# Two consecutive tokens per partition in a fused linear attention and soft mixture-of-experts kernel

## The chip, the cores and the metric

The kernel runs on one core of a Trainium2 chip. Time is device microseconds (us); a run counts as slow when it lies more than 1.5% above the fastest of the same kernel. Medians count all runs of a kernel, ratios its fast runs alone, so small differences are judged by the ratios. Profiles are one execution each; a span in a profile is some 1.8 us shorter than the timed value. In profiles PE is TensorE, PEld its weight loads, DVE VectorE, ACT ScalarE, POOL GpSimd, and SP the engine whose queue (SPq) issues the loads. Tiles lie in one of two on-chip memories, SBUF and PSUM; the kernel's matmuls write to PSUM. "Before" and "after" are the two versions of the kernel. A pair is the changed kernel's unit of 256 tokens, a chunk the earlier kernel's unit of 128.

## The reference

Shapes: r, k, v are 4 x 8 x 768 x 48 (batch, head, token, head dimension), f32; eight experts, four slots each, hidden width 1024. Cut to what matters:

```python
for t in range(S):                       # attention with a decaying state
    cur = einsum('bhd,bhe->bhde', u * k[t], v[t])
    y[t] = einsum('bhd,bhde->bhe', r[t], state + cur)
    state = w * state + einsum('bhd,bhe->bhde', k[t], v[t])
x = y as (3072 tokens) x (384)
logits = x @ phi                         # soft mixture of experts, 32 slots
d = softmax(logits, over tokens); slot_in = d.T @ x
slot_out[e] = relu(slot_in[e] @ w1[e]) @ w2[e]      # e = 0..7
return softmax(logits, over slots) @ slot_out
```

The softmax over tokens needs all tokens, so the experts can only start after the attention loop.

## The kernel before

The loop handles 24 chunks of 128 tokens, one token per partition. GpSimd multiplies r and k with powers of the decay and k with u; ScalarE copies v to bf16 and r into PSUM; TensorE transposes, computes 128x128 scores of each head, output and state; VectorE multiplies scores with the triangular mask, forms the diagonal term (ku, its sum, dv) and decays the state. All PSUM tiles are single, and in the timelines each engine ran its instructions in program order (VectorE from 60.51 us on: state multiply, ku, its sum, dv, mask multiplies). Weights of the experts come by sixteen transfers of 768 KB, issued from GpSimd in the iterations that W_AT names. Cuts are marked "# ...".

```python
def load_batch(b):                       # 192-byte rows: 48 f32 of one token and head
    # ...
    if b > 0:
        for t, (_, src) in zip(tiles, srcs):
            nc.sync.dma_start(out=t[:].rearrange("p h c d -> p (h c) d")[:, :, 0:D],
                              in_=src[b].rearrange("h (c p) d -> p (h c) d", p=C))
        return
    for c in range(nC):
        # one transfer of 128 tokens for each of r, k, v

def tables():
    for _ in range(C.bit_length() - 1):  # w to the power 128 by seven squarings
        nc.vector.tensor_mul(w_pd[:], w_pd[:], w_pd[:])
    for par in range(2):
        ps = slice(par * 64, par * 64 + 64)
        nc.vector.tensor_copy(wm[ps, :, par * D:(par + 1) * D],
                              w_pd[ps, :, None].to_broadcast([64, nP, D]))
    nc.vector.tensor_copy(phi_s[:], phi_f[:])

def mults(i):
    # ...
    nc.gpsimd.tensor_mul(rr[:, :, 0:D], r_b[:, :, c, 0:D], W_neg[:])
    nc.gpsimd.tensor_mul(kk[:, :, 0:D], k_b[:, :, c, 0:D], W_k3)
    nc.gpsimd.tensor_mul(ku[:], k_b[:, :, c, 0:D], u3)
    nc.scalar.copy(v_bf[:], v_b[:, :, c, 0:D])

def diag(i):
    nc.vector.tensor_mul(s["ku"][:], s["ku"][:], s["r_p"][:])
    # ... d: 8 sums per token, in PSUM
    nc.vector.tensor_reduce(d, s["ku"][:], axis=mybir.AxisListType.X, op=ALU.add)
    nc.vector.tensor_mul(dv[:], s["v"][:], d[:, :, None].to_broadcast([P, H, D]))

def att_a(i):
    for q in range(nP):
        for a in range(2):
            sl = slice(a * 64, a * 64 + 64)
            nc.tensor.matmul(at_p[a][:, q, :], t_s[sl, 1, q, :], t_s[sl, 0, q, :], # ...
    for a in range(2):
        nc.vector.tensor_mul(at_s[:, a, :, :], at_p[a][:], mask_ut[:, None, :].to_broadcast([P, nP, P]))
# att_b: dv and the state product into y_p, new state in sd_p; att_c: scores times v, x_t by ScalarE
# xt, lg: transposed x_t, logits, Exp; disp: dispatch sums into un_p; lexp_t: transposed logits

W_AT = [9, 10, 15, 15, 16, 16, 17, 18, 19, 20, 21, 22, 23, 24, 24, 24]
# ...
for i in range(nN + 3):                  # conditions on i left out
    att_a(i); mults(i + 2); trans(i + 1); att_b(i); r_copy(i + 1); xt(i - 1)
    disp(i - 2); att_c(i); diag(i + 1); lg(i - 1); lexp_t((i - 5) // G)
    # load_w for the entries of W_AT equal to i
# then the experts (up: h_p, down: so_p), the combination and twelve output transfers
```

The softmax here doesn't subtract the row's maximum and nothing guards it: scores larger than these inputs give would overflow.

Of the kernel before, what the change touches and what calls it, by code (L numbers as in the profile page):

```python
# [11 lines left out]
def kernel(  # L12
# [35 lines left out]
    nG = nN // G  # L48

# [3 lines left out]
    w2_all = wts.tile([P, E, nF, Dm], bf, name="w2_all")  # L53
    cst = ctx.enter_context(tc.tile_pool(name="cst", bufs=1))
    fill = cst.tile([P, 40], f32, name="fill")
    late = ExitStack()
    ld = late.enter_context(tc.tile_pool(name="ld", bufs=2))
# [3 lines left out]
    def load_batch(b):  # L61
        srcs = (("r_b", r), ("k_b", k), ("v_b", v))
        tiles = [ld.tile([P, H, nC, 64], f32, name=name, tag=name) for name, _ in srcs]
        loads[b] = tiles
        if b > 0:
            for t, (_, src) in zip(tiles, srcs):
                nc.sync.dma_start(out=t[:].rearrange("p h c d -> p (h c) d")[:, :, 0:D],  # L67
                                  in_=src[b].rearrange("h (c p) d -> p (h c) d", p=C))
            return
        for c in range(nC):  # L70
            for t, (_, src) in zip(tiles, srcs):
                nc.sync.dma_start(out=t[:, :, c, 0:D],  # L72
                                  in_=src[b, :, c * C:(c + 1) * C, :].rearrange("h p d -> p h d"))

    w_rep = cst.tile([P, H * D], f32, name="w_rep")
    nc.sync.dma_start(out=w_rep[:], in_=w.flatten().partition_broadcast(P))
    u_rep = cst.tile([P, H * D], f32, name="u_rep")
    nc.scalar.dma_start(out=u_rep[:], in_=u.flatten().partition_broadcast(P))
    load_batch(0)
# [6 lines left out]
    iotash = cst.tile([P, 1], mybir.dt.int32, name="iotash")  # L86
    nc.gpsimd.iota(iotash, pattern=[[0, 1]], base=-C, channel_multiplier=1)
    ishf = cst.tile([P, 1], f32, name="ishf")
    nc.vector.tensor_copy(ishf[:], iotash[:])
    ishf2 = cst.tile([P, 1], f32, name="ishf2")  # L90
    nc.vector.tensor_scalar(out=ishf2[:], in0=ishf[:], scalar1=-1.0, scalar2=-1.0,
                            op0=ALU.mult, op1=ALU.add)
    ident = cst.tile([P, P], bf, name="ident")
    make_identity(nc, ident)
    mask_ut = cst.tile([P, P], f32, name="mask_ut")
    make_upper_triangular(nc, mask_ut, val=1.0, diag=False)
# [6 lines left out]
    W_neg = cst.tile([P, H, D], f32, name="W_neg")  # L103
    nc.scalar.activation(out=warm[:], in_=warm[:], func=AF.Ln)
    nc.scalar.activation(out=w_rep[:], in_=w_rep[:], func=AF.Ln)
    nc.scalar.activation(out=W_neg[:].rearrange("p h d -> p (h d)"), in_=w_rep[:], func=AF.Exp, scale=ishf[:])  # L106
    nc.scalar.activation(out=w_rep[:], in_=w_rep[:], func=AF.Exp, scale=ishf2[:])

    wm = cst.tile([P, nP, D2], f32, name="wm")
    nc.vector.memset(wm[:], 0.0)  # L110
    ones = cst.tile([P, P], bf, name="ones")
    nc.vector.memset(ones[:], 1.0)
    phi_s = cst.tile([P, nM, ES], bf, name="phi_s")

    def tables():
        for _ in range(C.bit_length() - 1):
            nc.vector.tensor_mul(w_pd[:], w_pd[:], w_pd[:])
        for par in range(2):
            ps = slice(par * 64, par * 64 + 64)
            nc.vector.tensor_copy(wm[ps, :, par * D:(par + 1) * D],  # L120
                                  w_pd[ps, :, None].to_broadcast([64, nP, D]))
        nc.vector.tensor_copy(phi_s[:], phi_f[:])

    W_k3 = w_rep[:].rearrange("p (h d) -> p h d", h=H)
    u3 = u_rep[:].rearrange("p (h d) -> p h d", h=H)

    NB = 3
    rr_t, kk_t = [], []
    for i in range(NB):
        for lst, nm in ((rr_t, "rr"), (kk_t, "kk")):  # L130
            t = cst.tile([P, H, 64], bf, name=f"{nm}{i}")
            nc.vector.memset(t[:, :, D:64], 0.0)
            lst.append(t)
    st_t = [cst.tile([P, nP, D2], bf, name=f"st{i}") for i in range(2)]
# [3 lines left out]
    Lexp = cst.tile([P, nN, ES], bf, name="Lexp")  # L138
    LexpT = cst.tile([P, nG, P], bf, name="LexpT")
    rsum = cst.tile([P, nN], f32, name="rsum")  # L140
    rsum_r = cst.tile([P, nN], f32, name="rsum_r")

    def load_w(i):
        e = i // 2
        if i % 2 == 0:
            nc.gpsimd.dma_start(out=w1_all[:, e, :, :], in_=w1_ap[:, e, :, :])  # L146
        else:
            nc.gpsimd.dma_start(out=w2_all[:, e, :, :], in_=w2_ap[:, e, :, :])  # L148

    unsiT = cst.tile([P, nM, ES], bf, name="unsiT")  # L150
    csum_r = cst.tile([P, ES], f32, name="csum_r")

    with tc.tile_pool(name="wk", bufs=2) as wk, \
         tc.tile_pool(name="wk3", bufs=3) as wk3, \
         tc.tile_pool(name="wk4", bufs=4) as wk4, \
         tc.tile_pool(name="ps", bufs=1, space=bass.MemoryType.PSUM) as ps:
        un_p = ps.tile([P, nM + 1, ES], f32, name="un_p")
        st8 = {}

        def mults(i):  # L160
            b, c = divmod(i, nC)
            if b not in loads:
                load_batch(b)
            if c == 1 and 1 <= b < B - 1:
                load_batch(b + 1)
            r_b, k_b, v_b = loads[b]
            rr, kk = rr_t[i % NB], kk_t[i % NB]
            nc.gpsimd.tensor_mul(rr[:, :, 0:D], r_b[:, :, c, 0:D], W_neg[:])  # L168
            nc.gpsimd.tensor_mul(kk[:, :, 0:D], k_b[:, :, c, 0:D], W_k3)  # L169
            ku = wk.tile([P, H, D], f32, name="ku")  # L170
            nc.gpsimd.tensor_mul(ku[:], k_b[:, :, c, 0:D], u3)  # L171
            v_bf = wk3.tile([P, H, D], bf, name="v_bf")
            nc.scalar.copy(v_bf[:], v_b[:, :, c, 0:D])  # L173
            st8[i] = dict(rr=rr, kk=kk, ku=ku, v=v_bf)

        def r_copy(i):
            b, c = divmod(i, nC)
            r_p = ps.tile([P, H, D], f32, name="r_p")
            nc.scalar.copy(r_p[:], loads[b][0][:, :, c, 0:D])  # L179
            st8[i]["r_p"] = r_p  # L180

        def diag(i):
            b, c = divmod(i, nC)
            s = st8[i]
            nc.vector.tensor_mul(s["ku"][:], s["ku"][:], s["r_p"][:])  # L185
            sd_p = ps.tile([P, nP * D2 + H], f32, name="sd_p")
            s["sd"] = sd_p
            d = sd_p[:, nP * D2:nP * D2 + H]
            nc.vector.tensor_reduce(d, s["ku"][:], axis=mybir.AxisListType.X, op=ALU.add)  # L189
            dv = wk.tile([P, H, D], bf, name="dv")  # L190
            nc.vector.tensor_mul(dv[:], s["v"][:], d[:, :, None].to_broadcast([P, H, D]))  # L191
            s["dv"] = dv

        def trans(i):
            s = st8[i]
            t_p = ps.tile([P, 2, nP, P], bf, name="t_p")
            for a, nm in enumerate(("rr", "kk")):
                for q in range(nP):
                    nc.tensor.transpose(t_p[:, a, q, :],  # L199
                                        s[nm][:, 2 * q:2 * q + 2, :].rearrange("p h d -> p (h d)"), ident[:])  # L200
            t_s = wk.tile([P, 2, nP, P], bf, name="t_s")
            nc.scalar.copy(t_s[:], t_p[:])  # L202
            s["t"] = t_s

        def att_a(i):
            s = st8[i]
            t_s = s["t"]
            at_p = [ps.tile([P, nP, P], f32, name=f"at_p{a}") for a in range(2)]
            for q in range(nP):
                for a in range(2):  # L210
                    sl = slice(a * 64, a * 64 + 64)
                    nc.tensor.matmul(at_p[a][:, q, :], t_s[sl, 1, q, :], t_s[sl, 0, q, :],  # L212
                                     start=(q == 0), stop=(q == nP - 1), skip_group_check=True)
            at_s = wk.tile([P, 2, nP, P], bf, name="at_s")
            for a in range(2):
                nc.vector.tensor_mul(at_s[:, a, :, :], at_p[a][:],  # L216
                                     mask_ut[:, None, :].to_broadcast([P, nP, P]))
            s["at"] = at_s

        def att_b(i):  # L220
            b, c = divmod(i, nC)
            s = st8[i]
            y_p = ps.tile([P, H * D], f32, name="y_p")
            s["y"] = y_p
            nc.tensor.matmul(y_p[:], ident[:], s["dv"][:].rearrange("p h d -> p (h d)"),  # L225
                             start=True, stop=False, skip_group_check=True)
            if c > 0:
                for q in range(nP):
                    nc.tensor.matmul(y_p[:, q * D2:(q + 1) * D2], s["t"][:, 0, q, :], st_t[i % 2][:, q, :],
                                     start=False, stop=False, skip_group_check=True)  # L230
# [12 lines left out]

        x_of = {}

        def att_c(i):
            s = st8[i]
            y_p = s["y"]
            for a in range(2):
# [57 lines left out]
        for i in range(nN + 3):  # L307
            if i < nN:
                att_a(i)
# [116 lines left out]
```

## Time and profile before

| what | before |
|---|---|
| time, median of 3 runs | 154.82 us (153.78 to 155.56) |
| first mask multiply starts | 19.5 us |
| last mask multiply ends | 107.4 us |
| first expert matmul starts | 111.4 us |
| last expert matmul ends | 135.6 us |
| span ends | 153.2 us |

The first mask multiply marks the end of the preparation and the last one the end of the loop. From the page of the kernel before: busy us (share of the span) and count of each engine; TensorE's granted clock in tenths over 40 equal slices; the shares of the chain that ended last, by engine.

```profile
PE 86.6 (57%) x1433; PEld 65.3 (43%) x1433; DVE 98.2 (64%) x206; ACT 77.7 (51%) x162; POOL 86.2 (56%) x100
...
PEclk9999999998555899999999655999755555555555
...
DMA 38%; SPq 21%; POOL 12%; PE 10%; ACT 6%; DVE 4%; issue 4%; ACTq 0%; DVEq 0%; POOLq 0%
```

VectorE's 64% is an average over a loop in which it is full (busy 20.35 of the 21 us from 60 to 81 us) and a weight wait in which it has little to do (6.44 of the 29.8 us from 105 us on). DMA and the queue that issues it (SPq) are 59% of the chain. These two readings lead to different hopes for a change: cheaper transfers, or fewer VectorE microseconds.

### The profile page before, as it was taken

What the parts mean: (1) busy time and instruction counts of PE and PEld (TensorE: products, weight loads), DVE (VectorE), ACT (ScalarE), POOL (GpSimd) and SP (SyncE); (2) the same over time, 40 slices, a digit from 0 to 9 for tenths busy, and PEclk for the clock granted to TensorE, in tenths of its full rate; (3) what the DMA queues carried; (4) which work ended last, traced back from release to release, by engine and by line L of the source; (5) the groups of instructions that cost most, each with busy time, mean ns of one, the idle gap of its engine ahead of it and who ended that gap; (6) DMA issues with size and microseconds to landing.
All of it is one profiled execution on the core that took longest, in us unless ns stands there. A gap on an engine that the chain in (4) does not pass through costs nothing.

```text
span 153.2 us, 3605 instructions
## 1 busy us (share of the span) xinstructions
PE 86.6 (57%) x1433; PEld 65.3 (43%) x1433; DVE 98.2 (64%) x206; ACT 77.7 (51%) x162; POOL 86.2 (56%) x100
## 2 busy tenths in 40 slices
PE   0035059782778878768783789785396522259100
PEld 0014047561656755546562577563296411132000
DVE  3009998992788899999994988999232100028610
ACT  3446126853767887897928777864300000018510
POOL 7089917784577789998899999995000000000000
PEclk9999999998555899999999655999755555555555
DMA  3999998964389929996899999999999999907994
GB/s 65 196 216 202 220 223 254 278 198 117 98 231 285 267 58 155 205 284 186 250 297 209 207 206 208 209 209 207 209 207 208 207 210 202 171 1 278 400 399 157
DMA packets 47873, 32.13 MB, mean 210 GB/s; under 512 B 19424, under 2 KB 44768, under 8 KB 47856
## 3 DMA queue, kind: packets, MB, share of 16 engines
q0 software_dynamic: 11616, 12.63, 49.0%
q1 hardware_dynamic: 36096, 19.07, 44.8%
q10 hardware_dynamic: 144, 0.20, 0.7%
q8 instruction: 11, 0.18, 0.5%
q14 instruction: 6, 0.05, 0.1%
HBM read 39.77 MB, written 4.72 MB: 290 GB/s over the span
## 4 chain that ended last, share of the span: by engine, by line
DMA 38%; SPq 21%; POOL 12%; PE 10%; ACT 6%; DVE 4%; issue 4%; ACTq 0%; DVEq 0%; POOLq 0%
DMA w_all<-in_moe_w_dram 20%; DMA v_b<-in_v_dram 14%; SPq L72 12%; SPq L67 10%; DMA out_dram<-o_s 4%; POOL rr L168 3%; PE t_p L199 3%; POOL kk L169 2%; POOL ku L171 2%; POOL w_all L148 2%; ACT t_s L202 2%; PE at_p L212 2%; ACT xt_s L267 1%; POOL w_all L146 1%; ACT r_p L179 1%
## 5 line engine op out<-in xcount | busy, mean ns | idle before, releaser
L202 ACT COPY t_s<-t_p 128x1024 bf16<-128x1024 bf16 x24 | 24.3, 1011 | 13.7 <-PE t_p L199 13.7
L171 POOL TENSOR_TENSOR ku<-k_b,u_rep 128x384 f32<-128x384 f32 x24 | 24.0, 1001 | 12.8 <-DVE sd_p L189 12.0
L216 DVE TENSOR_TENSOR at_s<-at_p,mask_ut 128x512 bf16<-128x512 f32 x48 | 30.7, 681 | 0.0
L168 POOL TENSOR_TENSOR rr<-r_b,W_neg 128x384 bf16<-128x384 f32 x24 | 24.1, 1004 | 4.4 <-ACT W_neg L106 4.2
L169 POOL TENSOR_TENSOR kk<-k_b,w_rep 128x384 bf16<-128x384 f32 x24 | 24.0, 1001 | 1.3 <-PE sd_p L238 0.7
L185 DVE TENSOR_TENSOR ku<-ku,r_p 128x384 f32<-128x384 f32 x24 | 13.1, 547 | 16.3 <-POOL ku L171 8.9
L393 ACT ACTIVATE o_s<-o_p,rsum_r 128x384 f32<-128x384 f32 x12 | 6.4, 584 | 29.9 <-PE o_p L387 27.9
L173 ACT CAST v_bf<-v_b 128x384 bf16<-128x384 f32 x24 | 12.2, 507 | 10.5 <-DMA v_b<-in_v_dram 10.5
L252 PE MATMUL y_p<-v_bf,at_s 128*128 128x48 bf16 x192 | 12.5, 194 | 7.5 <-DVE at_s L216 7.5
L199 PE MATMUL t_p<-ident,rr 128*128 128x128 bf16 x96 | 11.4, 254 | 9.3 <-POOL rr L168 9.3
L256 ACT CAST x_t<-y_p 128x384 bf16<-128x384 f32 x24 | 11.6, 484 | 5.7 <-PE y_p L252 5.7
L189 DVE TENSOR_REDUCE sd_p<-ku 128x8 f32<-128x384 f32 x24 | 13.5, 561 | 0.8
L191 DVE TENSOR_TENSOR dv<-v_bf,sd_p 128x384 bf16<-128x384 bf16 x24 | 13.3, 554 | 0.8
L267 ACT COPY xt_s<-xl_p 128x384 bf16<-128x384 bf16 x24 | 11.5, 481 | 4.0 <-PE xl_p L265 3.9
L225 PE MATMUL y_p<-dv,ident 128*128 128x384 bf16 x24 | 9.4, 394 | 6.5 <-DVE dv L191 6.3
L274 PE MATMUL xl_p<-phi_s,xt_s 128*128 128x32 bf16 x72 | 5.9, 185 | 12.2 <-ACT xt_s L267 11.7
L212 PE MATMUL at_p<-t_s 64*128 64x128 bf16 x192 | 11.4, 251 | 2.1 <-ACT t_s L202 2.1
L252 PEld LDWEIGHTS <-at_s 128*128 128x128 bf16 x192 | 8.5, 103 | 9.5 <-DVE at_s L216 8.6
L242 DVE TENSOR_TENSOR st<-sd_p,wm 128x384 bf16<-128x384 f32 x20 | 11.0, 550 | 1.6 <-PE sd_p L238 1.4
L199 PEld LDWEIGHTS <-rr 128*128 128x128 bf16 x96 | 6.5, 110 | 12.5 <-POOL rr L168 9.7
L179 ACT COPY r_p<-r_b 128x384 f32<-128x384 f32 x24 | 11.7, 489 | 0.0
L199 PE MATMUL t_p<-ident,kk 128*128 128x128 bf16 x96 | 11.5, 254 | 0.3 <-POOL kk L169 0.3
(66 smaller groups left out, 171.0 us busy)
## 6 DMA issues: line engine op xcount, KB each, us to landing
w_all<-in_moe_w_dram POOLq DMA_DIRECT2D x16, 768.0 KB, 15.0
out_dram<-o_s SPq DMA_DIRECT2D x12, 384.0 KB, 4.1
r_b<-in_r_dram SPq DMA_DIRECT2D x6, 192.0 KB, 3.6
k_b<-in_k_dram SPq DMA_DIRECT2D x6, 192.0 KB, 3.7
v_b<-in_v_dram SPq DMA_DIRECT2D x6, 192.0 KB, 3.7
u_rep<-in_u_dram ACTq DMA_DIRECT2D x1, 192.0 KB, 5.3
w_rep<-in_w_dram SPq DMA_DIRECT2D x1, 192.0 KB, 5.0
phi_f<-in_moe_phi_dram POOLq DMA_DIRECT2D x1, 48.0 KB, 4.6
```

The costliest lines, as they stand in the source:

```text
L67: nc.sync.dma_start(out=t[:].rearrange("p h c d -> p (h c) d")[:, :, 0:D], in_=src[b].rearrange("h (c p) d -> p (h c) d", p=C))
L72: nc.sync.dma_start(out=t[:, :, c, 0:D], in_=src[b, :, c * C:(c + 1) * C, :].rearrange("h p d -> p h d"))
L168: nc.gpsimd.tensor_mul(rr[:, :, 0:D], r_b[:, :, c, 0:D], W_neg[:])
L169: nc.gpsimd.tensor_mul(kk[:, :, 0:D], k_b[:, :, c, 0:D], W_k3)
L171: nc.gpsimd.tensor_mul(ku[:], k_b[:, :, c, 0:D], u3)
L189: nc.vector.tensor_reduce(d, s["ku"][:], axis=mybir.AxisListType.X, op=ALU.add)
L191: nc.vector.tensor_mul(dv[:], s["v"][:], d[:, :, None].to_broadcast([P, H, D]))
L199: nc.tensor.transpose(t_p[:, a, q, :], s[nm][:, 2 * q:2 * q + 2, :].rearrange("p h d -> p (h d)"), ident[:])
L202: nc.scalar.copy(t_s[:], t_p[:])
L212: nc.tensor.matmul(at_p[a][:, q, :], t_s[sl, 1, q, :], t_s[sl, 0, q, :], start=(q == 0), stop=(q == nP - 1), skip_group_check=True)
L216: nc.vector.tensor_mul(at_s[:, a, :, :], at_p[a][:], mask_ut[:, None, :].to_broadcast([P, nP, P]))
L252: nc.tensor.matmul(y_p[:, h * D:(h + 1) * D], s["at"][:, a, q, :], s["v"][:, h, :], start=False, stop=(a == 1 and q == nP - 1), skip_group ...
```

## The change

The intent: put two consecutive tokens of a head on one partition, so that a row of a load is 384 bytes instead of 192 and one load covers 256 tokens; keep chunks of 128 tokens, now on 64 partitions with two tokens each, so that scores are computed by 64x64 tiles of the array; hold logits per pair only, which frees memory for four sets of loads and for weights that come early. GpSimd's and ScalarE's instructions become twice as wide and half as many. Core of the diff, cuts marked "# ...":

```diff
+        t = ld.tile([P, H, J, D], f32, name=name)              # J = 2, four buffers
+        nc.sync.dma_start(out=t[:].rearrange("p h j d -> p h (j d)"),
+                          in_=src[b, :, i * TS:(i + 1) * TS, :].rearrange("h (p j) d -> p h (j d)", j=J))
 # ... decay tables and masks for both tokens of a partition
-            nc.gpsimd.tensor_mul(rr[:, :, 0:D], r_b[:, :, c, 0:D], W_neg[:])
+            nc.gpsimd.tensor_mul(rr[:, :, :, 0:D], jh(r_l), W_n[:])
 # ... kk, ku and v_bf likewise: 768 instead of 384 wide
+        def kur(n, j):
+            nc.vector.tensor_mul(s["ku"][:, j, :, :], s["ku"][:, j, :, :], s["rp"][:])
 # ... diag: one sum and one dv for 768 columns
-                    nc.tensor.matmul(at_p[a][:, q, :], t_s[sl, 1, q, :], t_s[sl, 0, q, :],
+                for g in range(2):
+                    for a in range(2):
+                        sl = slice(a * 64, a * 64 + 64)
+                        nc.tensor.matmul(at_p[a][g * HF:(g + 1) * HF, q, :], kT[sl, q, g, j, :],
+                                         rT[sl, q, g, :, :].rearrange("p j c -> p (j c)"),
+                                         start=True, stop=True, tile_position=(a * 64, g * HF), # ...
 # ... y_open, inter, state, intra: y, state and scores times v on 64 rows each
 # ... logits and Exp per pair; dispatch sums collected in un_a by VectorE; row sums by a matmul (blk)
-        W_AT = [9, 10, 15, 15, 16, 16, 17, 18, 19, 20, 21, 22, 23, 24, 24, 24]
+        W_AT = [0, 1, 1, 1, 1, 1, 1, 1, 1, 1, 1, 2, 2, 2, 2]     # now a count per iteration
-        for i in range(nN + 3):
 # ...
+        for n in range(nS + 2):
+            live = n < nS
+            load(n + 3)
 # ...
+            disp(n - 2, s_now)
+            att(n, 0)
+            mults(n + 2)
+            trans(n + 1, "rr")
+            r_copy(n + 1, 0)
+            kur(n + 1, 0)
+            att(n, 1)
+            trans(n + 1, "kk")
+            r_copy(n + 1, 1)
+            kur(n + 1, 1)
+            if live:
+                y_open(n)
+                inter(n, 0)
+                state(n, 0)
+            xt(n - 1)
+            if live:
+                inter(n, 1)
+                state(n, 1)
+                intra(n)
+            lg(n - 1)
+            diag(n + 1)
+            if 2 <= n and n % 2 == 0 and n // 2 <= nG:
+                lexp_t(n // 2 - 1)
+            load_w(W_AT[n])
```

## The prediction

> **What bounds the kernel now.** I read the chain that ended last first, then the stretch table, then the timeline of single engines. First the chain of waits of the kernel before (start in us, length in us, what):
>
> ```profile
> 104.61 30.10 DMA w_all<-in_moe_w_dram
> 134.76 0.81 PE so_p L360 x24
> 135.60 0.22 DVE soT L363
> 135.86 0.51 PE sr_p L375 x3
> ...
> 138.58 6.89 DMA out_dram<-o_s x2
> ```
>
> From 104.6 to 134.8 us nothing but the expert weights decides; from the last expert's matmuls (134.76) to the end (153.2) pass 18.4 us. The stretch table (stretch, its length, busy us of PE, PEld, DVE, ACT, POOL, the granted clock, the DMA share, GB/s) shows two regimes:
>
> ```profile
> 22.00:31.00 9.00, 7.38 (x98) 5.73 (x97) 8.16 (x16) 6.43 (x14) 6.95 (x8) 1.00 0.88 253
> 60.00:81.00 21.00, 15.60 (x270) 11.54 (x267) 20.35 (x39) 15.58 (x36) 19.89 (x22) 1.00 1.00 241
> 105.00:134.80 29.80, 12.81 (x403) 11.83 (x400) 6.44 (x24) 1.73 (x5) 0.49 (x1) 0.57 1.18 198
> ```
>
> In the attention loop VectorE is busy 20.35 of 21 us (97%): that stage is VectorE-bound, with GpSimd at 95%. Then come 30 us of weights at about 200 GB/s with idle engines. The last chunk leaves VectorE at about 107 us, so the end is: loop, then a wait for weights that were issued only from chunk 9 (56.7 us) on, then 18.4 us. VectorE inside the loop, one chunk of 128 tokens (start us, us):
>
> ```profile
> 60.98 0.55 DVE L185 TENSOR_TENSOR ku<-ku,r_p 128x384 f32<-128x384 f32 x1
> 61.56 0.56 DVE L189 TENSOR_REDUCE sd_p<-ku 128x8 f32<-128x384 f32 x1
> 62.15 0.55 DVE L191 TENSOR_TENSOR dv<-v_bf,sd_p 128x384 bf16<-128x384 bf16 x1
> 62.62 1.28 DVE L216 TENSOR_TENSOR at_s<-at_p,mask_ut 128x512 bf16<-128x512 f32 x2
> 63.82 0.54 DVE L185 TENSOR_TENSOR ku<-ku,r_p 128x384 f32<-128x384 f32 x1
> ```
>
> There is no gap: start to start .58, .59, .47, 1.20, and .47 for the state multiply where there is one (60.51 to 60.98), 3.3 us a chunk. TensorE and ScalarE keep ahead of it.
>
> [...]the seven 128x4 squarings of w_pd, all in SBUF, while GpSimd multiplies back to back (min/median/max ns):
>
> ```profile
> L117 DVE TENSOR_TENSOR w_pd<-w_pd x7: 240/918/932, 12.8 to 17.9; 128x4 f32<-128x4 f32 x7
> ```
>
> Alone one takes 240 ns; the others last as long as one GpSimd multiply (0.95 us start to start). [...]In the trace 8 score matmuls at 64 rows start at 61.20 and the 128-row transposes at 61.53; within the group they are some 31 ns apart, so about 0.08 us is left for the change. [...]the page's row of granted clock agrees (0.9 or 0.5), with two half-clock stretches of some 12 us inside the loop.
>
> **The change, part by part.** *Loads.* 14.16 MB of r, k, v. At 253 GB/s (above) they are 56 us of DMA[...]. Weights are 60.5 us (12.6 MB at 208), output 12.4 (4.7 MB at 380); the sum was 129 of 153 us. The weights now start with the second iteration instead of at 57 us, one per iteration, so at the loop's end most have landed. GpSimd issues the last eight right after the multiplies for the last pair, two iterations before the end: 8 × 3.8 = 30 us, while two to three iterations, the tail and the first experts last as long. The 23 us between the first expert (111) and 134.8 us mostly go, but the experts, formerly hidden, then run bare: 16 groups of 24 matmuls at 0.64 us (timeline, 112.71 to 113.36), 10.3 us.
>
> *Prologue.* GpSimd's multiplies become 768 wide, so 1.9 us each, and start as before at about 8.8 us after the decay table. ku(0) is ready near 15 us, the two ku products end near 16.9. Then the seven squarings come: five each wait out a GpSimd multiply of 1.9 us, to 25 us, and with the casts (0.7) and the 768-wide reduce and multiply (1.9) the first mask multiply comes at 28 us, against 19.5 before: +8.5 us.
>
> *VectorE per pair* (256 tokens): four mask multiplies 2.40, two ku 1.16, reduce .99, dv .87, two states .94, the sum of un_a .2, LexpT .12: 6.7 us against 2 × 3.3. Nothing is saved. GpSimd: 5.75 + 0.85 for a weight issue = 6.6. ScalarE about 5.7.
>
> *The order of waits is what changes.* All PSUM tiles are single, and each engine runs in program order. I laid one iteration out by hand from durations in the trace, full clock, with t=0 at the last state matmul of the previous pair. Drain plus semaphore is 0.2.
> - intra: 32 matmuls at 30 ns (4 took 0.26 us, of which 0.17 is the drain): to 0.96; ScalarE copies x_t, 768 wide, from 1.18 (0.70), Exp to 2.1.
> - The dispatch matmuls head the next iteration and need that Exp: 2.13 to 2.4. Before, they stood late in the following chunk. Then 16 score matmuls of 64x64 (0.56) and 8 transposes (0.48): the first transposed copy (1.01 us, 1024 wide) starts at 3.84, and only behind it in ScalarE's queue comes r_copy, 4.74 to 5.23.
> - VectorE: ku product 5.28, the second mask pair 5.86 to 7.06. The second ku waits for the other r_copy, behind the second transposed copy: 7.40. State multiply 7.98 to 8.53.
> - TensorE: inter and state of the second half wait for that multiply: 8.58 to 9.45. End of the iteration.
>
> So 9.45 us, 8.84 where a batch ends (no second state): 9.25 on average, with VectorE busy for 6.7. At half clock the matmuls in the chain cost about 1.7 us more (intra .3, score .45, transposes .35, the rest .6); with a third of the loop at half clock, as before, 9.8 us.
>
> *Sum.* First mask 28.0; pair 0's last state at 34.4; pair 1 without dispatch 8.6, 43.0; nine more at 9.8: 131. Last pair, with its transposes, logits and dispatch: 13.5, so 144.7. Experts to the start of the last group 9.6: 154.3. Then 18.4 as before: 172.7 of span; the timed median lies 1.6 over the span: 174. I take 172[...].
>
> **Rivals.** (a) *The DMA gain shows.* For: the chain is 38% DMA, and loads get cheaper and weights earlier. If VectorE stayed as full as it was, an iteration is 6.7 us: 28 + 12 × 6.7 + 6 + 9.6 + 18.4 = 142, timed 144. Against: that needs every handover above hidden, and with single PSUM tiles and r_copy behind the transposed copies there is nothing left for VectorE to run meanwhile. (b) *TensorE becomes the bound:* the matmuls and loads grow (score and intra doubled in number). At full clock an iteration issues some 6.1 us, at half about 10, so with the clock low throughout: 11 us, timed 185.[...] (c) *The tail is weight-bound again:* the last eight issue at about 113 us, landing near 145; the last expert needs its weights at 154. Hidden, and only if the loop is quick does it bind.
>
> **Range and chances.** The iteration decides: a microsecond each way is 10 to 12 us. At 8.5 us [...]I get 160, at 10.8 (clock low) 184. To win by 2% (under 151.7) an iteration would have to be under about 7.7 us, close to VectorE's floor of 6.7; to tie, under some 8.2. Faster 0.06, same 0.09, slower 0.85; 80% between 159 and 183.
>
> **What would show it.** The squarings at about 1.9 us each, and the first mask multiply near 28 us; mask pairs of one parity 9 to 10 us apart; VectorE under 80% busy in the loop, idle ahead of the ku products (ScalarE's r_copy), the second state multiply and the first mask multiply (TensorE); TensorE idle ahead of the dispatch for Exp; no DMA wait ahead of the experts; loads well above 253 GB/s when alone. I am wrong if VectorE stays near 95%, if tiles overlap so much that intra and scores nearly vanish, or if the clock stays low throughout.

## The result, and the profile after

After: **176.13 us** median of 4 runs (174.54 to 178.67), beside 155.19 us (153.78 to 156.01) for the kernel before. The ratio is 1.133, 95% interval 1.117 to 1.148. A ratio here is the mean time of one kernel's fast runs over that of the other's fast runs of the same rounds, so it is not quite the ratio of the medians quoted. All ratios below are to the kernel before, run beside the experiment.

| piece of the span, us | before | after | difference |
|---|---|---|---|
| until the first mask multiply | 19.5 | 27.0 | +7.5 |
| first to last mask multiply | 87.8 | 108.5 | +20.7 |
| until the first expert matmul | 4.0 | 8.1 | +4.1 |
| experts | 24.2 | 10.0 | -14.2 |
| end: combination and output | 17.6 | 19.9 | +2.2 |
| span | 153.2 | 173.4 | +20.2 |

The same three rows of the page after:

```profile
PE 108.8 (63%) x1927; PEld 80.3 (46%) x1927; DVE 103.3 (60%) x205; ACT 74.1 (43%) x114; POOL 81.2 (47%) x64
...
PEclk9999999999995555857985555555576575555555
...
PE 44%; DVE 22%; ACT 14%; DMA 7%; SPq 5%; issue 4%; ACTq 0%; DVEq 0%
```

DMA and its queue fell from 59% of the chain to 12%; the chain now runs through TensorE, VectorE and ScalarE in turn. The chip got what the change meant to give, cheap transfers (299 GB/s from 8 to 20 us, where it was 215), and the time went to handing work from engine to engine.

The squarings of w_pd (count, min/median/max ns, first and last start):

```profile
L149 DVE TENSOR_TENSOR w_pd<-w_pd x7: 161/1061/1739, 17.5 to 24.3; 128x4 f32<-128x4 f32 x7
```

The stretch table after, for five iterations from first mask multiply to first mask multiply (columns as in the prediction):

```profile
26.99:36.39 9.40, 6.82 (x105) 5.11 (x105) 6.35 (x11) 3.50 (x6) 5.10 (x4) 1.00 0.45 119
45.60:54.02 8.42, 5.23 (x119) 3.81 (x118) 6.65 (x14) 5.24 (x8) 8.00 (x6) 0.91 1.03 209
54.02:63.90 9.88, 8.23 (x127) 6.15 (x127) 6.64 (x12) 5.24 (x8) 4.54 (x4) 0.50 1.21 269
82.61:92.22 9.61, 5.72 (x129) 4.29 (x128) 7.11 (x14) 5.17 (x8) 6.68 (x6) 0.89 1.09 245
92.22:102.12 9.90, 8.89 (x132) 6.52 (x132) 6.66 (x12) 5.24 (x8) 5.16 (x4) 0.50 0.73 119
```

In the iterations of 9.9 us VectorE (third busy figure) has about 6.6 us of work, 67%, where it was at 97%. In the iteration from 82.61 us TensorE has only 5.72 us of work and VectorE 7.11, no wait ends with a DMA, and it still takes 9.61 us: no engine is full in it. VectorE's timeline in the iteration that starts at 63.90; in brackets, how long it was idle before the instruction and who released it:

```profile
63.90 1.29 DVE L250 TENSOR_TENSOR at_s<-at_p,mask 128x512 bf16<-128x512 f32 x2
66.41 0.56 DVE L208 TENSOR_TENSOR ku<-ku,rp 128x384 f32<-128x384 f32 x1 [1.23 <-ACT rp L202]
66.88 1.28 DVE L250 TENSOR_TENSOR at_s<-at_p,mask 128x512 bf16<-128x512 f32 x2
68.51 0.56 DVE L208 TENSOR_TENSOR ku<-ku,rp 128x384 f32<-128x384 f32 x1 [0.34 <-ACT rp L202]
...
70.58 0.56 DVE L297 TENSOR_TENSOR st<-s_p,wm 128x384 bf16<-128x384 f32 x1 [1.02 <-PE s_p L292]
```

Both ku products wait for ScalarE's r_copy, and the second state multiply for TensorE: the gaps that the prediction listed, in its order. The list of waits sums them over the execution (engine and line, whom it waited for: us, times, longest):

```profile
DVE ku L208 <- ACT rp L202: 19.6, 21, 4.2
...
PE at_p L245 <- DVE at_s L250: 11.7, 17, 6.0
...
DVE st L297 <- PE s_p L292: 11.4, 9, 1.6
```

Last, TensorE's timeline, of which only the groups of sixteen 64x64 score matmuls and of eight transposes are shown:

```profile
44.72 0.42 PE L245 MATMUL at_p<-t_rr,t_kk 64*64 64x128 bf16 x16
45.07 0.62 PE L227 MATMUL t_p<-ident,rr 128*128 128x128 bf16 x8
...
63.21 0.64 PE L245 MATMUL at_p<-t_rr,t_kk 64*64 64x128 bf16 x16
```

The same sixteen matmuls take 0.42 us in one place and 0.64 us in another. I read from this the rate at which the array really ran. In the stretch from 54.02 us, recorded at a clock of 0.50, the row of sixteen (63.21) takes 0.64 us: that length I call the half rate, 0.42 us the full one. Eleven iterations have such a row of sixteen; it is 0.64 us in nine of them and 0.42 us in two (44.72 and 82.15 us). So most of this loop ran at the half rate, including the first iterations, for which the record of granted clock still says 1.00 (26.99 to 36.39 us, with a row of 0.64 us at 34.59). I take the length of a known group for the better witness. Nor does a run's mean granted clock sort the times: of the runs of a_rows192 (below), those at 0.884 and 0.893 took 179.14 and 178.74 us, the one at 0.632 took 177.95.

### The profile page after: what moved, and what is told of

Same layout as the page of the kernel before. It is cut to its first block, busy times and chain, and to the rows that moved or that the text cites. A ratio compares the mean times of both kernels' runs of the same rounds, so it can differ in the third digit from the quotient of the medians.

```text
span 173.4 us, 4471 instructions
## 1 busy us (share of the span) xinstructions
PE 108.8 (63%) x1927; PEld 80.3 (46%) x1927; DVE 103.3 (60%) x205; ACT 74.1 (43%) x114; POOL 81.2 (47%) x64
## 4 chain that ended last, share of the span: by engine, by line
PE 44%; DVE 22%; ACT 14%; DMA 7%; SPq 5%; issue 4%; ACTq 0%; DVEq 0%
PE t_p L227 10%; PE s_p L292 6%; SPq L72 5%; PE at_p L245 4%; DMA out_dram<-o_s 4%; ACT t_rr L230 4%; PE y_p L272 4%; DVE w_pd L149 4%; DVE at_s L250 4%; DVE dv L217 3%; PE xl_p L329 3%; ACT x_t L315 3%; PE so_p L447 3%; DVE rp L215 3%; PE h_p L435 3%
## 5 line engine op out<-in xcount | busy, mean ns | idle before, releaser
L189 POOL TENSOR_TENSOR kk<-k_l,W_k 128x768 bf16<-128x768 f32 x12 | 21.7, 1808 | 27.3 <-PE s_p L292 27.3
L250 DVE TENSOR_TENSOR at_s<-at_p,mask 128x512 bf16<-128x512 f32 x48 | 30.8, 684 | 2.6 <-PE at_p L245 2.4
L245 PE MATMUL at_p<-t_rr,t_kk 64*64 64x128 bf16 x384 | 17.8, 294 | 12.8 <-DVE at_s L250 11.7
L208 DVE TENSOR_TENSOR ku<-ku,rp 128x384 f32<-128x384 f32 x24 | 13.3, 554 | 19.8 <-ACT rp L202 19.6
L188 POOL TENSOR_TENSOR rr<-r_l,W_n 128x768 bf16<-128x768 f32 x12 | 22.1, 1843 | 5.5 <-DVE W_n L125 5.3
L191 POOL TENSOR_TENSOR ku<-k_l,u_rep 128x768 f32<-128x768 f32 x12 | 21.7, 1812 | 2.8 <-DVE rp L215 2.8
L230 ACT COPY t_rr<-t_p 128x1024 bf16<-128x1024 bf16 x12 | 12.1, 1012 | 16.6 <-PE t_p L227 16.5
L297 DVE TENSOR_TENSOR st<-s_p,wm 128x384 bf16<-128x384 f32 x20 | 11.1, 556 | 11.4 <-PE s_p L292 11.4
L230 ACT COPY t_kk<-t_p 128x1024 bf16<-128x1024 bf16 x12 | 12.1, 1012 | 11.8 <-PE t_p L227 11.8
L227 PE MATMUL t_p<-ident,kk 128*128 128x128 bf16 x96 | 11.4, 294 | 6.1 <-ACT t_rr L230 5.4
L292 PE MATMUL s_p<-v_bf,kk 64*128 64x96 bf16 x160 | 14.5, 254 | 0.0
L202 ACT COPY rp<-r_l 128x384 f32<-128x384 f32 x24 | 11.7, 488 | 5.1 <-DVE dv L217 4.4
L176 POOL DMA_DIRECT2D w_all<-in_moe_w_dram x16 | 13.6, 856 | 0.0
```

The source lines that it names most:

```text
L176: nc.gpsimd.dma_start(out=dst[:, e, :, :], in_=src[:, e, :, :])
L188: nc.gpsimd.tensor_mul(rr[:, :, :, 0:D], jh(r_l), W_n[:])
L189: nc.gpsimd.tensor_mul(kk[:, :, :, 0:D], jh(k_l), W_k[:])
L191: nc.gpsimd.tensor_mul(ku[:], jh(k_l), u_rep[:, None, :, :].to_broadcast([P, J, H, D]))
L208: nc.vector.tensor_mul(s["ku"][:, j, :, :], s["ku"][:, j, :, :], s["rp"][:])
L227: nc.tensor.transpose(t_p[:, q, :, j, :], s[nm][:, j, 2 * q:2 * q + 2, :].rearrange("p h d -> p (h d)"), ident[:])
```

## The experiments

Twelve kernels ran; all gave correct results. They ran in several rounds, on more than one chip, each beside the kernel before. The theory: the loss is the order of waits (with single buffers and in-order queues VectorE is left with nothing to run), plus squarings that wait for GpSimd (up to 1.74 us each). The rivals: TensorE's extra matmuls or its clock; the wider rows or the early weights as causes or as gains.

### a_sq: squarings with one operand in PSUM

```diff
-            nc.vector.tensor_mul(w_pd[:], w_pd[:], w_pd[:])
+            nc.vector.tensor_copy(q_p, w_pd[:])            # q_p in PSUM
+            nc.vector.tensor_mul(w_pd[:], w_pd[:], q_p)
```

> The changed kernel, with one operand of each of the seven squarings of w_pd in PSUM (a small copy ahead of each). Contention theory: the squarings take about 0.2 us each instead of up to 1.74, the group with its copies under 3 us instead of 6.95, the first mask multiply comes near 22.5 us instead of 27.0, and all of it shows in the time, since the prologue is serial: about 4.5 us less (176 to 171.5). Rival, that the squarings are slow for another reason (the latency of dependent small instructions): they stay at 1 us and nothing changes. Rival, that the start is hidden behind something later: the mask multiply is early and the time stays.

Measured: 176.75 us, ratio 1.133 (1.122 to 1.145): no gain. The seven copies and seven products together took 2.7 us, as expected, but the next two copies of the table, both operands in SBUF, now ran while GpSimd was still multiplying. VectorE's timeline of this kernel:

```profile
20.54 3.54 DVE L155 COPY wm<-w_pd 64x192 f32<-64x192 f32 x2
```

In the changed kernel the same two copies took 0.52 us (from 24.47 us), since GpSimd was done by then (its multiply ended at 23.8 us). The contention had only moved to the next instruction that could meet it.

### a_sq2: the table copies read PSUM too, and ScalarE casts phi

```diff
-            nc.vector.tensor_copy(wm[sl, ...], w_pd[sl, :, None].to_broadcast([64, nP, D]))
+            nc.vector.tensor_copy(wm[sl, ...], q_p[sl, :, None].to_broadcast([64, nP, D]))
-        nc.vector.tensor_copy(phi_s[:], phi_f[:])
+        nc.scalar.copy(phi_s[:], phi_f[:])
```

> As a_sq, and the two copies that spread the result into wm read it from PSUM, and the cast of phi goes to ScalarE, so that VectorE has no instruction left in the prologue that works from SBUF to SBUF beside GpSimd. In a_sq the wait only moved from the squarings (6.95 to 2.7 us) to these copies (3.54 us), and the first mask multiply gained only 0.9 us. Contention theory: the whole group takes about 3.5 us, the first mask multiply comes near 23 us (27.0 before), and the time falls by about 4 us, to 172. Rival, that it is hidden later: the time stays within 1.5 us of 176.

Measured: 172.14 us (170.37 to 174.16), ratio 1.097 (1.087 to 1.107). The copies beside the same GpSimd work:

```profile
20.73 0.72 DVE L156 COPY wm<-s_p 64x192 f32<-64x192 f32 x2
```

The first mask multiply came at 23.2 us instead of 27.0, and the time fell by 4.0 us. So of the 7.5 us lost in the preparation, some 3.8 were contention between VectorE and GpSimd over SBUF (0.2 us of this is the cast of phi, which left VectorE).

### a_disp: the dispatch matmuls later in TensorE's queue

```diff
-            disp(n - 2, s_now)
             att(n, 0)
 # ...
             att(n, 1)
+            lexp_sum(n // 2 - 1 if n % 2 else -1)   # row sums of the previous logits group
+            disp(n - 2, s_now)
```

> The changed kernel, with the dispatch matmuls of pair n-2 moved behind the second score group, and the row-sum matmul of the transposed logits moved into the next iteration. The same instructions in another order. Theory of the order of waits: TensorE no longer waits for Exp (0.8 us an iteration) nor for VectorE's LexpT copy (1.1 us in every second one) ahead of the score matmuls; the even iterations shorten by about 1.2 us, the odd ones by 0.3 to 0.5, since VectorE's reduce and multiply are there nearly as late; in all 6 to 9 us less than 176. Rival, TensorE's throughput is the bound: the work is the same, so the time stays within 2 us.

Measured: 172.96 us (171.35 to 174.65), ratio 1.100 (1.092 to 1.109): 3.2 us off the median, which counts two slow runs, and 4.1 us between the means of the fast runs; 6 to 9 were hoped for. TensorE's wait for Exp ahead of the dispatch fell from 4.3 to 0.7 us in sum, and the one for the transposed logits from 4.4 to 0.4, but other waits took up most of it: TensorE's wait for the mask multiplies ahead of a score group grew from 11.7 to 17.6 us in sum.

### a_rcopy: r_copy ahead of the transposed copies in ScalarE's queue

```diff
-            trans(n + 1, "rr")
             r_copy(n + 1, 0)
+            trans(n + 1, "rr")
 # ... the same for "kk" and r_copy(n + 1, 1)
```

> The changed kernel, with each r_copy ahead of the transposed copy in ScalarE's queue instead of behind it. Theory of the order of waits: the idle ahead of the ku products (19.6 us in 21 waits) mostly goes; at full clock the iteration shortens by about 0.8 us, at half clock hardly, as TensorE's state matmuls then end at the same time as the second ku; in all 3 to 6 us less. If ScalarE's queue alone were the bound: 10 us and more. Rival, TensorE's throughput: within 1 us of 176.

Measured: 173.10 us (171.44 to 175.24), ratio 1.107 (1.097 to 1.116): 3.0 us off the median. Its list of waits (the profile fell on a slow run, so only the pattern is used):

```profile
DVE st L297 <- PE s_p L292: 23.6, 20, 1.6
```

The wait of ku for r_copy fell from 19.6 us (21 times) to 4.8 us (2 times, one of 4.3 us), and the wait of the state multiply for TensorE rose from 11.4 us (9 times) to 23.6 us (20 times). One gap was closed and the next one in the chain opened: that is how some 15 us of waits gave 3 us of time.

### a_rows192: rows of 192 bytes in the changed kernel

```diff
-            t = ld.tile([P, H, J, D], f32, name=name)
-            nc.sync.dma_start(out=t[...], in_=src[...].rearrange("h (p j) d -> p h (j d)", j=J))
+            t = ld.tile([P, J, H, D], f32, name=name)
+            for j in range(J):
+                nc.sync.dma_start(out=t[:, j, :, :], in_=src[...].rearrange("h (p j) d -> j p h d", j=J)[j])
```

> The changed kernel with rows of 192 bytes: each load of a pair split into two, one token of each partition at a time, 72 loads instead of 36, the tile laid out by token. Theory: loads are hidden in the changed kernel, so the time stays within 2 us of 176, though the loads at the start run near 215 to 250 GB/s instead of 300 to 312. Rival, DMA matters in the loop: 5 us or more are lost.

Measured: 178.94 us (177.95 to 179.96), ratio 1.148 (1.140 to 1.156), by the medians 2.8 us more than the changed kernel, a little outside the expectation; the intervals of the two ratios overlap, so the difference is not clear of the noise. Waits of ScalarE for loads of v grew from 4.6 us (2 times) to 10.6 us (4 times). In the changed kernel the longer rows are nearly hidden, hence worth next to nothing; a small remainder, if there is one, was not taken apart.

### a_all2: the three repairs together

The edits of a_sq2, a_disp and a_rcopy in one kernel.

> a_sq2, a_disp and a_rcopy together. If their gains are waits in one chain they add up: 4 + 3.5 + 2.5 us measured or expected apart, and as each removal leaves the next wait exposed a little more together than apart: 163 to 167. If TensorE at half clock is what is left (the state multiply waiting for s_p in nearly every iteration), the gains of the two orders overlap and only 168 to 170 comes out. In neither case does it reach the kernel before (155), because the experts run bare behind the loop and VectorE still waits.

Measured: 161.23 us (158.59 to 163.09), ratio 1.021 (1.012 to 1.030). At the limit of 2% the verdict against the kernel before is unclear; against the changed kernel it is much faster. Between the means of the fast runs the three together gained 16.3 us, where alone they gained 4.0, 4.1 and 3.1. By the ratios it is some 17 us against 5.5, 5.0 and 4.0; the intervals are too wide to show that the repairs give more than their sum. Two of its iterations in the stretch table:

```profile
48.20:56.04 7.84, 5.62 (x134) 4.46 (x133) 6.62 (x12) 5.37 (x9) 5.54 (x5) 1.00 1.22 258
...
81.36:91.08 9.72, 9.54 (x139) 7.04 (x138) 6.61 (x14) 5.25 (x8) 6.10 (x5) 0.50 0.93 175
```

At full clock the iteration takes 7.84 us, of which VectorE works 6.62. At half clock TensorE seems busy for 9.54 of 9.72 us, which spoke for the rival that TensorE is the bound. The next order of instructions was to tell the two apart.

### b_wpart and b_best: the kernel before with earlier weights

Is the gain just the early weights, to be had without the new layout? b_wpart gives the kernel before a spread schedule, b_best fits weights into stretches with a low DMA share and has the squarings through PSUM.

```diff
-        W_AT = [9, 10, 15, 15, 16, 16, 17, 18, 19, 20, 21, 22, 23, 24, 24, 24]
+        W_AT = [3, 5, 7, 9, 11, 13, 15, 17, 19, 21, 21, 21, 23, 23, 24, 24]     # b_wpart
+        W_AT = [4, 5, 9, 9, 10, 15, 15, 16, 16, 17, 18, 19, 20, 21, 22, 23]     # b_best
```

> The kernel before, with one part of the change alone: the weights are issued from the fourth chunk on, one every two chunks as in the change (one per pair), the last four at chunks 23 and 24. It costs no instruction. If the 23 us of weights at the end were all there was to win, the loop would end as before at 107, the experts run bare for 10 us and the end comes at 140. But r, k and v (56 us at 192 bytes) and weights (60 us) then share the loop, which gives some 116 us of DMA in some 100 us: I expect the chunks to wait for v at batch borders, the loop to end near 115 to 120, and 143 to 150 in all. Rival, that the order of the weights was tuned just so and early weights only delay the loads: 155 or more.

> The kernel before with two small things: the squarings and their copies with an operand in PSUM as in a_sq2, and the weights shifted so that they fill the two holes in the DMA's row (33 to 42 and 53 to 60 us): two at chunks 4 and 5, the rest two to three issues earlier. Theory: the weights end some 8 us earlier from the shift and 3 us earlier from the quicker start: 144 to 148, faster than both kernels. Rival: the loads of batch 1 or 2 are delayed by the weights beside them and take back half of it: 150 to 152.

Measured: b_wpart 161.51 us (157.61 to 163.31; only one of its four runs counts as fast, so no ratio is given), b_best 157.84 us (156.03 to 158.67), ratio 1.008 (0.999 to 1.017). Both expectations of a gain were missed. The chain of b_wpart, then of b_best, has the reason:

```profile
47.75 16.12 DMA v_b<-in_v_dram
```

```profile
74.89 20.99 DMA v_b<-in_v_dram
```

A load of v on which the loop depends took 16 and 21 us beside the earlier weights; in the chain of the kernel before, such loads took 10 and 11 us. So transfers are scarce in the loop of the kernel before as well (DMA share 1.00 from 60 to 81 us), and its late weights cost less than these earlier ones.

### a_order: a new order in TensorE's queue

a_all2, plus: the first half's output and state matmuls ahead of the second score group, dispatch at the end of the iteration, the transposed logits in the next one.

```diff
             kur(n + 1, 0)
+            if live:
+                y_open(n); inter(n, 0); state(n, 0)
             att(n, 1)
-            disp(n - 2, s_now)
 # ...
-            if live:
-                y_open(n); inter(n, 0); state(n, 0)
             xt(n - 1)
 # ...
             diag(n + 1)
-            if 2 <= n and n % 2 == 0 and n // 2 <= nG:
-                lexp_t(n // 2 - 1)                  # now after att(n, 0) of the next iteration
+            disp(n - 2, s_now)
```

> The combined kernel (squarings from PSUM, dispatch later, r_copy ahead of the transposed copies) plus a new order in TensorE's queue: the identity matmuls, inter and state of the first half stand ahead of the second score group instead of behind it, so that VectorE has the first state multiply to run while the second ku product waits; the dispatch goes to the end of the iteration, the logit transposition into the following one. Theory (the order of waits on single buffers is the loss, VectorE's 6.7 us per pair is the floor under it): full-clock iterations fall from 7.84 to about 7.0 us, half-clock ones from 9.2 to 9.7 to about 8.7, the loop from 95 us to about 86, and the time from 161 to 150 to 154 us, at or just under the kernel before. Rival (after the earlier edits TensorE's work at half clock is the limit, 8.3 to 9.5 us busy of 9.2 to 9.7): only full-clock iterations gain, and the time is 157 to 160 us.

Measured: **148.40 us** (147.13 to 148.78, 6 runs, all fast), ratio 0.958 (0.953 to 0.963): faster than both kernels, by 4% over the kernel before and by some 28 us over the changed one, with the layout of the change untouched. The stretch table, four usual iterations (the second ends a batch) and one that is not:

```profile
22.83:29.55 6.72, 6.40 (x105) 4.87 (x104) 6.17 (x11) 4.45 (x6) 6.72 (x5) 1.00 0.91 242
37.02:42.98 5.96, 5.02 (x126) 3.93 (x126) 5.89 (x11) 5.25 (x9) 5.94 (x5) 1.00 1.15 276
50.94:57.25 6.31, 5.41 (x136) 4.27 (x135) 6.28 (x13) 5.24 (x9) 6.29 (x5) 1.00 1.19 248
63.98:70.29 6.31, 5.52 (x138) 4.55 (x137) 6.28 (x11) 4.83 (x8) 3.91 (x4) 0.97 1.19 241
70.29:82.97 12.68, 7.15 (x135) 5.50 (x134) 6.73 (x14) 5.76 (x9) 7.88 (x6) 0.73 1.15 234
```

In the iteration from 50.94 us VectorE is busy 6.28 of 6.31 us, and GpSimd, with the issue of a weight, 6.29. VectorE's timeline in it has no gap:

```profile
50.94 1.28 DVE L254 TENSOR_TENSOR at_s<-at_p,mask 128x512 bf16<-128x512 f32 x2
52.14 0.54 DVE L212 TENSOR_TENSOR ku<-ku,rp 128x384 f32<-128x384 f32 x1
52.60 0.55 DVE L301 TENSOR_TENSOR st<-s_p,wm 128x384 bf16<-128x384 f32 x1
53.07 1.28 DVE L254 TENSOR_TENSOR at_s<-at_p,mask 128x512 bf16<-128x512 f32 x2
```

Between the two mask pairs VectorE now has a ku product and a state multiply to run. The first iteration, whose matmul groups ran at the half rate (score groups of 0.64 us), still took only 6.72 us. So at half rate TensorE does not have to set the pace at 8 us and more. How far the half rate costs something in the later, fuller iterations this kernel can't tell, since it spent less of its loop there; that three things moved at once also leaves their shares open.

Was it the order, or the full rate that came more often with it? Iterations of the same pair and at nearly the same rate tell. The seventh pair, at full rate for most of the iteration in both kernels, took 9.61 us (from 82.61) in the changed kernel and 6.31 (from 63.98) here; the third, the end of a batch and likewise at full rate, 8.42 (from 45.60) and 5.96 (from 37.02); the first, at the half rate in both, 9.40 and 6.72. That is 2.5 to 3.3 us an iteration for the order at equal rate; over eleven iterations 27 to 36 us (an estimate from these three), which covers the 24 us by which the loop got shorter, even with the 5.4 us for which a_order's loop stood for a load. So the order itself brought the gain, and the rate is not needed to explain it.

| piece of the span, us | before | after | a_order |
|---|---|---|---|
| until the first mask multiply | 19.5 | 27.0 | 22.8 |
| first to last mask multiply | 87.8 | 108.5 | 84.2 |
| until the first expert matmul | 4.0 | 8.1 | 7.7 |
| experts | 24.2 | 10.0 | 13.3 |
| end | 17.6 | 19.9 | 19.0 |
| span | 153.2 | 173.4 | 147.0 |

### a_order_w: the same with the weights spread earlier

```diff
-        W_AT = [0, 1, 1, 1, 1, 1, 1, 1, 1, 1, 1, 2, 2, 2, 2]
+        W_AT = [2, 1, 1, 2, 1, 1, 2, 1, 1, 1, 3, 0, 0, 0, 0]
```

> The same with the sixteen weight transfers spread earlier (2, 1, 1, 2, 1, 1, 2, 1, 1, 1, 3 in the first eleven iterations; the last three instead of eight at the end). If a shorter loop makes the experts wait for the last eight weights (8 transfers at 3.8 us are 30 us, issued some two iterations before the end), this is 2 to 5 us faster than the new order alone. If the loop still ends later than the weights land, it is the same within 1 us, or up to 2 us slower through loads that share their DMA time with weights.

Measured: 161.13 us (160.60 to 163.78), ratio 1.042 (1.037 to 1.046), 12.7 us slower than a_order; neither branch of the expectation had that size. Two pieces of its chain, from the profile of a slow run:

```profile
26.41 21.89 DMA k_l<-in_k_dram
...
55.81 22.04 DMA v_l<-in_v_dram
```

Loads took 22 us beside four weights each (issued from 25.25 to 38.43 us and from 51.96 to 65.22), and three sets of loads in flight did not cover that. The slack in the weight schedule is small on this side: four weights more in the first seven iterations, and the loop stops for its loads.

### a_order_rows: the same with rows of 192 bytes

The edit of a_rows192 on a_order.

> The new order with the loads cut to rows of 192 bytes again (72 loads instead of 36, tiles held by token; nothing else). In the changed kernel itself this cost at most 3 us, since its loads were hidden. In the new order VectorE is at its floor in most iterations, the DMA share is 0.8 to 1.2 from 4 to 121 us, one load already stops the loop for 5 us and the experts wait 2 us for weights. Theory (with the order repaired, the transfers are what is left, so the gain of the longer rows now shows): the loads need 14.16 MB at 253 instead of 299 to 312 GB/s, 9 to 11 us more DMA, and the time is 155 to 160 us, 7 to 11 more than 148.4. Rival (the order alone does it, rows are hidden still): 148 to 151 us.

Measured: 172.48 us (170.96 to 175.57), ratio 1.099 (1.089 to 1.109), 24 us more than a_order by the medians and 22 by the ratios, over twice what was expected. The stretch from 8 to 20 us, in which only loads of r, k and v are under way (last column: GB/s), of a_order and then of this kernel:

```profile
8.00:20.00 12.00, 2.05 (x16) 1.62 (x17) 5.85 (x31) 5.73 (x10) 10.62 (x6) 1.00 1.09 293
```

```profile
8.00:20.00 12.00, 1.04 (x8) 0.88 (x9) 3.23 (x16) 3.48 (x7) 10.68 (x6) 1.00 1.06 204
```

14.16 MB at 204 GB/s are 69 us, at 293 GB/s 48 us: 21 us, near what was measured; a byte of the longer rows took 204/293 = 0.70 of the time. ScalarE waited 36.5 us for loads of v, against 10.3 us in a_order. So the gain that the change was made for is real, and large, but shows only once the handovers are out of the way: at most some 3 us in the changed kernel, 24 us here. The edit also doubles the number of transfers and sets their rows 384 bytes apart, so the row length is not the only thing that differs, and the 204 GB/s are a little under the 215 that the kernel before reached with 192-byte rows in its first loads (8 to 20 us).

### a_order_late: two weights fewer ahead of the load that stopped the loop

```diff
-        W_AT = [0, 1, 1, 1, 1, 1, 1, 1, 1, 1, 1, 2, 2, 2, 2]
+        W_AT = [0, 1, 1, 1, 1, 1, 0, 0, 1, 1, 1, 2, 2, 2, 2]      # the rest at the end
```

> The new order with two weight transfers taken out of iterations 6 and 7, ahead of the load of v that stopped the loop for 5.4 us at 69 us, and added to the eight at the end. If the loop's stall is what costs, this is 3 to 5 us faster, 143.5 to 145.5 us. If the sum of transfers is the limit (they run without a break from 4 to 121 us), the stall moves to the experts, which wait 2 us for weights already: 147 to 150 us.

Measured: 150.22 us (149.35 to 153.06), ratio 0.961 (0.954 to 0.969), beside 0.958 (0.953 to 0.963) for a_order: the same. Its chain:

```profile
97.43 30.60 DMA w_all<-in_moe_w_dram
```

The stop of 5.4 us in the loop is gone, and the experts wait for weights until 128 us instead. This fits the second branch of the expectation, that the sum of the transfers is what limits this version; it is not shown beyond this one shift, and a_order_w shows that a bad place for the weights costs far more.

## Why the prediction was right

The prediction said slower, 172.0 us within 159 to 183; 176.13 was measured.

- **Preparation.** Predicted first mask multiply 28.0 us, measured 27.0. The squarings did wait for GpSimd, up to 1.74 us each (put at 1.9; GpSimd's multiply is 1.8). a_sq2 confirms the cause by taking it away. The working has a slip: five waits of 1.9 us from 16.9 end at 26.4, not at 25. The 240 ns read as the time of a squaring alone was too long as well: the shortest here took 0.16 us. Most squarings took less than put (median 1.06 us, the whole group 6.95), which made up for the slip.
- **Order of waits as the loss.** The gaps came where they were listed, ahead of the ku products, the second state multiply and the dispatch; the one named ahead of the first mask multiply was small (2.4 us in sum). Order, on the same arithmetic and the same tiles, gives most of the 28 us between the changed kernel and a_order; the squarings gave 4 of them. At equal rate it is worth 2.5 to 3.3 us an iteration (see a_order).
- **VectorE's floor.** Put at 6.7 us per pair; a_order has iterations of 6.3 us with VectorE full.
- **Iteration length.** Predicted 9.8 us; the mean from the second pair on was 9.6. Three terms of that sum were mis-sized and made up for each other, so that the two agree this well is partly luck. First, the small tiles: sixteen 64x64 scores were put at 0.56 us and took 0.35 at full rate until the next group started (44.72 to 45.07), 0.57 at the half rate (53.33 to 53.90). Two iterations ran mostly at full rate: the end of a batch (45.60 to 54.02) took 8.42 us, predicted 8.84; a full one (82.61 to 92.22) took 9.61, predicted 9.45, with the wait of the next point in it. Second, the surcharge of the half rate: put at 1.7 us; an end of a batch at half rate took 9.68 us (102.12 to 111.80), 1.3 more. Third, "with a third of the loop at half clock, as before": nine of eleven score groups ran at the half rate, and whole iterations of 9.9 us were recorded at 0.50 with TensorE busy for 8.2 to 8.9 of them. Why it was so much more than a third, no run here shows. The 0.2 us put for drain plus semaphore is an estimate; in the kernel before, eight transposes start at 61.53 some 60 ns apart, and the copy that reads them starts at 62.25, 0.24 us after they are all issued.
- **A wait not foreseen.** Every second iteration TensorE waited up to 1.1 us for VectorE's copy of the transposed logits ahead of the dispatch (4.4 us in sum). It is small, and a_order moved it.
- **Experts.** No wait for weights, as predicted; 9.6 us to the last group, as predicted. The time from the last iteration to the experts and the end of the kernel were each some 2 us off.
- **Rivals.** (a) that the DMA gain shows at 144 us, was wrong for the changed kernel and nearly right for a_order (148.4): the stated condition, every handover hidden, was the right one, but the remark that single PSUM tiles leave VectorE nothing to run was too strong. The order could be changed without another buffer. (b) TensorE as the bound, was close in half-rate iterations of the changed kernel (8.9 of 9.9 us busy), and an order that keeps VectorE full leaves 5.0 to 7.2 us of it in the five iterations shown. At full rate TensorE was busy for only 5.7 of 9.6 us of the changed kernel's iteration, which was hardly faster for it, and at equal rate the new order took 2.5 to 3.3 us off. So TensorE was not the bound, though the half rate made the waits in the chain longer (1.3 us in an iteration that ends a batch).

## What to carry to other kernels

When a change makes instructions fewer and wider, write down for one iteration what each engine has left to run, in program order, while it waits; the bound may move from an engine to the handovers, and repairs of these are best tried together, since each alone uncovers the next wait (here 4.0, 4.1 and 3.1 us alone, 16.3 together). A gain in a transfer that is hidden is worth nothing until the rest is quick enough to need it (at most some 3 us here, 24 us there), so a layout should be judged after its order is repaired. And early prefetch was not free: beside four weights issued too early, loads on which the loop stood took 22 us (6.4 us was the median load of that kernel), and the kernel was 12.7 us slower.
